# An order pinned, loads moved, a search moved and two priorities set in an attention-and-mixer kernel

## The chip, the cores and the metric

The kernel runs on one core of a Trainium2 chip. The metric is the device time of one execution in microseconds (us), as a median of several runs. Names in use below: PE is TensorE (matrix products), DVE is VectorE, ACT is ScalarE, POOL is GpSimd, and SP is SyncE, which issues most DMAs.

## The reference

For each of eight batches, an attention with two parts is computed from q, k and v (8 heads, 576 positions, width 64), and its result x goes through two pairs of products with a relu between, one along the positions and one along the channels:

```python
B, H, S, D = q.shape              # 8, 8, 576, 64
q_d = q.reshape(B, H, Sd, 4, D).mean(axis=3)      # likewise k_d, v_d; Sd = 144
out_d = sm_attn(q_d, k_d, v_d)                    # softmax attention, pooled
out_up = np.repeat(out_d, 4, axis=2)
mask = np.abs(pos[:, None] - pos[None, :]) < 4    # local attention
out_local = softmax(where(mask, scale * q @ k.T, -1e9)) @ v
x = (out_up + out_local), as (B, S, 512)

h = np.maximum(x.T @ w_tok1, 0.0) @ w_tok2        # (512,576)(576,256), (256,576)
u = x + h.T
h2 = np.maximum(u @ w_ch1, 0.0) @ w_ch2           # (576,512)(512,1536), (1536,512)
return u + h2
```

## The kernel before

The products run in 16-bit pairs: a float32 operand is split into a high and a low half after scaling by the largest value found, and three matmuls take the place of one. Each batch passes through these steps: loads of q, k (tiles `qk`), v (tiles `vr`, eight pieces of 72 x 512) and the windows of v (`vw`); pooling of q and k on POOL (lines 513 to 521); for each piece of v a square on ACT whose accumulated sum goes into `vm` (line 484) and two additions on POOL into `vd` (lines 487, 488); `value_scale`, which searches the largest of `vm` (DVE, a transposition and a broadcast on PE, DVE again: lines 649 to 658, 307 to 317); the pooled attention (sd, pd, td, ad, od) and the local attention (sc, P, pT, av); the position products (t1, hid, t2), which leave u; then the channel products. u is scaled and split into `uh` (lines 755, 757), the first channel product makes h, the second makes c2, and line 1025 adds it into u, which goes out.

Batches 0 and 1 take the first channel product directly (`c1_...`, 12 chunks for each of two column ranges, ranges 0 and 1). From batch 2 on, `product7` makes it with seven block products instead of eight, for six pairs of chunks: products P, Q and R with operands named a11, s1, s2, a12, s4, s3 and a22 go into three PSUM banks (m0, m1, m2). ACT copies three of them out (x1, m5, u2: line 903, in `plain`), DVE adds later ones onto those (lines 945, 949, 954), and ACT's relu and DVE's rest put the results into h (lines 910, 916, in `leave` and `rests`). The seven products need sums and differences of the channel weights, which `weight_sums` (lines 973 to 1002) makes once while batch 1 runs: for each of six pairs four additions (line 984) and four subtractions (line 991) on DVE, four casts and four subtractions on POOL (lines 993, 994), and two stores to DRAM (`sums0` to `sums5`), which batch 2 begins to read.

What sets the order: the preparation of the weights, batch 0, and part of batch 1 and of the loading of batches 1 and 2 is laid out by `drive`, which weighs planned durations, inside a stretch where the framework keeps the written order. All that follows is written by the loop at lines 1119 to 1163: each product step of PE with some work for the next batch beside it. The framework's scheduler then puts each engine's instructions into an order of its own, by dependences and priority; an instruction is free to move ahead unless `tc.keep_in_program_order` holds it. Every engine, and SP's queue, then works through its list in that order.

Tiles come from pools with a number of slots each. A tag "w" has four slots, one tile each, which `slot` picks in turn outside of `drive`; inside `drive` it returns the slot in use last. Pieces of v of batches 2 and later, and the tiles pd and ptd of the pooled attention, are in these slots. The loading of v stands thus:

```python
early = {0: 8, 1: 5}.get(st.b, 0)
for i in range(8):
    if i >= early:
        fetch(i)
    t = ts.pop(i)
    nc.scalar.activation(dump, t..., AF.Square, ..., accum_out=st.vm[:, i:i + 1])   # line 484
    nc.gpsimd.tensor_add(...); nc.gpsimd.tensor_add(st.vd..., ...)                  # lines 487, 488
```

Of the kernel before, what the change touches and what calls it, by code (L numbers as in the profile page):

```python
# [13 lines left out]
AF = mybir.ActivationFunctionType  # L14
# [14 lines left out]
LIVE = 3  # L29
# [14 lines left out]
def tile_ups_attention_mixer(ctx, tc, qk, vw, vr, w1, w2, c1, c2, out):  # L44
# [410 lines left out]
    def load_v(st):  # L455
# [17 lines left out]

        early = {0: 8, 1: 5}.get(st.b, 0)
        for i in range(early):
            yield step("S", ISSUE, *([("mixed", 0)] if st.b and i == 0 else []))
            fetch(i)
        for i in range(8):
            pr, g = divmod(i, 2)
            if i >= early:  # L480
                fetch(i)
            t = ts.pop(i)
            e = yield step("A", 0.7, at=arrives[i])
            nc.scalar.activation(dump, t.rearrange("p r c -> p (r c)"), AF.Square, scale=2.0 ** -20, accum_out=st.vm[:, i:i + 1])  # L484
            make(("vm", st.b, i), e)
            e = yield step("G", 1.25)
            nc.gpsimd.tensor_add(t[:, 0:2], t[:, 0:2], t[:, 2:4])  # L487
            nc.gpsimd.tensor_add(st.vd[:, g, 2 * pr:2 * pr + 2, :D], t[:, 0].rearrange("p (h d) -> p h d", d=D),
                                 t[:, 1].rearrange("p (h d) -> p h d", d=D))
            make(("v", st.b, i), e)  # L490
# [328 lines left out]
    def attention(st):  # L819
        todo = [pooled(st, pr) for pr in range(4)] + [local(st, t) for t in range(len(TILES))]  # L820
        yield from together(todo, LIVE)

# [4 lines left out]
    def ahead(b):  # L827
# [6 lines left out]
        yield from load_v(st)  # L834
        yield from value_scale(st)
        if b == 1:
# [44 lines left out]
    def product7(st, steps):  # L881
# [19 lines left out]
        def plain(src, name, engine):  # L901
            t = T([128, HS], F32, "tm", f"{name}{b}_{p}")
            nc.scalar.copy(t, src[:, :HS])
            return t
# [3 lines left out]
        def leave(src, r, i, h):  # L908
            o = h[:, i, :, HS * r:HS * r + HS]
            nc.scalar.activation(o[:, 0], src, AF.Relu)  # L910
            later.append((src, o))

        def rests():
            while later:
                src, o = later.pop(0)
                nc.vector.scalar_tensor_tensor(o[:, 1], src, 0.0, o[:, 0], ALU.max, ALU.subtract)

# [4 lines left out]
        for p in range(NP):  # L922
# [21 lines left out]
            product(Q, "a12", weights(fa, 1), True, True)  # L944
            nc.vector.tensor_tensor(x1, x1, Q[:, :HS], ALU.add)
            leave(x1, 0, 0, h)
            yield step("P", us, ("uh", b, "s4"))
            product(R, "s4", weights(fb, 1), False, True)
            nc.vector.tensor_tensor(u2, u2, R[:, :HS], ALU.add)  # L949
            rests()  # L950
            leave(u2, 0, 1, h)
            yield step("P", us, ("uh", b, "s3"))
            product(P, "s3", weights(0, 0, t123, 2), False, False)
            nc.vector.tensor_tensor(m5, m5, P[:, :HS], ALU.add)
            rests()
# [17 lines left out]
    def weight_sums():  # L973
# [4 lines left out]
        for p in range(NF // 2):  # L978
            fa, fb = C1.fin[2 * p], C1.fin[2 * p + 1]
            y = {}  # L980
            for n, f, o in (("a1", fa, 0), ("b1", fb, 0), ("b2", fb, 256), ("a2", fa, 256)):
                yield step("V", 0.42, gates[p])
                y[n] = T([128, 256], F32, "tm", f"{n}_{p}")
                nc.vector.tensor_tensor(y[n], f[:, 0, o:o + 256], f[:, 1, o:o + 256], ALU.add)
            if p == 0:
                ts12 = T([128, 2, 2, 256], F16, "uh", "ts12")
                ts3 = T([128, 2, 256], F16, "uh", "ts3")
            for x, z, o in (("b1", "a1", ts12[:, 0]), ("b2", "b1", ts3), ("b2", "a1", ts12[:, 1]), ("a2", "b2", fb[:, :, 0:256])):
                yield step("V", 0.42)
                to = {("b1", "a1"): "a1", ("b2", "b1"): "b1", ("b2", "a1"): "b2", ("a2", "b2"): "a2"}[x, z]  # L990
                nc.vector.tensor_tensor(y[to], y[x], y[z], ALU.subtract)
                yield step("G", 1.5)
                nc.gpsimd.tensor_copy(o[:, 0], y[to])
                nc.gpsimd.tensor_sub(o[:, 1], y[to], o[:, 0])
                if o is ts3:
# [216 lines left out]
```

## Time and profile before

| | us |
|---|---|
| median of three runs | 961.62 (960.66 to 961.94) |
| the profiled execution | 963.37 |
| its span in the trace | 961.6 |
| PE busy | 892.8 (93%) |
| DVE, ACT, POOL busy | 538.3, 424.7, 300.2 |

The page lists for each engine how long it was busy, and for groups of instructions how long the engine had been idle before them and whose work ended that. Where PE is busy nearly always, the table by stage is the first to be read: the length of a stage less PE's busy time is what PE waited, and the column PEclk is the mean clock granted to it, 1.00 being the full 2.4 GHz and 0.50 the lower level of 1.2 GHz. The stages are: to 145 us weights and batch 0; to about 215 batch 0's second channel product; 215 to 287 batch 1's first channel product (column range 0, then 1); 287 to 332 its second; then for each batch from 2 on some 50 to 57 us of block products and some 52 us of the second product, with the next batch's attention and position products beside them; batch 2 starts at 347, batch 7 at 890.

### The profile page before, as it was taken

The page shows a single profiled execution, that of the slowest core. Times are in us where ns is not written, and L with a number is a line of the kernel's source. Part 1 is how long each engine was busy: PE and PEld are TensorE (multiplying, and loading weights), DVE is VectorE, ACT ScalarE, POOL GpSimd, SP SyncE. Part 2 cuts the span into 40 slices and gives each one's busy share as a digit, 9 for nine tenths or more (in the row PEclk, how much of TensorE's full clock was granted, in tenths as well). Part 3 has the DMA queues.
Part 4 walks back from the last instruction along what each step waited for, and adds up shares of the span by engine and source line. Part 5 has one row for each costly group of instructions (what it writes and reads, how often), then busy time and mean ns, then how long its engine had stood idle before and what let it go on. Part 6 is the DMA issues. An engine that isn't in the chain of part 4 may idle for free.

```text
span 961.6 us, 26341 instructions
## 1 busy us (share of the span) xinstructions
PE 892.8 (93%) x11218; PEld 660.7 (69%) x11218; DVE 538.3 (56%) x1287; ACT 424.7 (44%) x1004; POOL 300.2 (31%) x457
## 2 busy tenths in 40 slices
PE   7877899997889989999999999899999999999998
PEld 3544678676667757767777768667777768767786
DVE  7789886436772266623765266633755266624631
ACT  4755673434351156622664156522655155423520
POOL 5898940415674021342024121241015120002000
PEclk9768999998999979999999999999999999999999
DMA  9584331511225112250135102260135211100200
GB/s 269 171 276 143 120 80 44 170 45 39 71 80 168 42 41 75 84 173 19 41 108 168 53 29 79 75 180 18 41 107 157 57 36 52 53 20 19 65 27 32
DMA packets 35143, 84.87 MB, mean 88 GB/s; under 512 B 4273, under 2 KB 15537, under 8 KB 33777
## 3 DMA queue, kind: packets, MB, share of 16 engines
q1 hardware_dynamic: 32464, 80.82, 28.1%
q10 hardware_dynamic: 2560, 2.36, 0.9%
q8 instruction: 88, 1.44, 0.6%
q14 instruction: 31, 0.25, 0.1%
HBM read 69.01 MB, written 11.80 MB: 84 GB/s over the span
## 4 chain that ended last, share of the span: by engine, by line
PE 73%; DVE 16%; ACT 5%; issue 3%; DMA 1%; POOL 1%; ACTq 0%; POOLq 0%; DVEq 0%; SPq 0%
PE c L124 32%; PE t L124 10%; PE P L124 9%; PE R L124 4%; PE av L636 3%; PE ad L567 3%; PE sc L600 2%; PE t L702 2%; PE Q L124 2%; PE busy L168 2%; PE pT L623 2%; PE td L558 2%; PE sd L539 1%; DVE CX L239 1%; DVE uh L757 1%
## 5 line engine op out<-in xcount | busy, mean ns | idle before, releaser
L124 PE MATMUL c<-h,CX 128*128 128x320 f16 (+1 forms) x2304 | 310.0, 286 | 3.0 <-DVE u L949 2.0
L124 PEld LDWEIGHTS <-CX 128*128 128x128 f16 x2304 | 221.1, 98 | 66.9 <-issue 6.1
L124 PEld LDWEIGHTS <-CW 128*128 128x128 f16 x1440 | 137.9, 99 | 55.2 <-issue 17.7
L487 POOL TENSOR_TENSOR vr<-vr 72x256 f32<-72x256 f32 x64 | 52.6, 821 | 196.2 <-ACT dump L484 189.5
L1025 DVE SCALAR_TENSOR_TENSOR u<-c,io,u 128x256 f32<-128x256 f32 (+1 forms) x64 | 32.8, 513 | 95.9 <-PE c L124 95.7
L124 PE MATMUL c<-uh,CW 128*128 128x256 f16 (+1 forms) x576 | 82.3, 295 | 1.7 <-DVE h L878 1.7
L729 ACT ACTIVATE u<-t,down 128x256 f32<-128x256 f32 (+1 forms) x64 | 29.9, 498 | 121.1 <-PE t L124 121.1
L771 POOL TENSOR_TENSOR s<-u,u 128x288 f32<-128x288 f32 x12 | 9.3, 796 | 234.4 <-ACT u L729 234.4
L124 PEld LDWEIGHTS <-t 128*128 128x128 f16 x648 | 62.4, 99 | 23.6 <-issue 7.9
L731 DVE TENSOR_REDUCE umx<-u 128x1 f32<-128x256 f32 (+1 forms) x64 | 27.8, 451 | 89.0 <-ACT u L729 89.0
L513 POOL TENSOR_TENSOR qs<-qk 128x288 f32<-128x288 f32 x56 | 39.3, 701 | 94.5 <-DMA qk<-in_qk_dram 90.9
L680 DVE SCALAR_TENSOR_TENSOR xh<-x,back,xh 128x512 f16<-128x512 f32 (+1 forms) x40 | 33.0, 825 | 57.3 <-ACT xh L678 56.2
L124 PE MATMUL t<-xh,W 128*128 128x512 f16 (+1 forms) x240 | 60.1, 386 | 2.0 <-DVE xh L680 2.0
L124 PE MATMUL t<-W,hid 128*128 128x256 f16 (+1 forms) x384 | 60.2, 289 | 0.4
L641 ACT ACTIVATE x<-av,up 128x512 f32<-128x512 f32 (+1 forms) x40 | 27.3, 683 | 41.8 <-PE av L636 35.2
L484 ACT ACTIVATE dump<-vr 72x512 uint8<-72x512 f32 x64 | 40.0, 624 | 12.5 <-DMA vr<-in_vr_dram 11.8
L567 PE MATMUL ad<-vd,ptd 72*72 72x65 f32 x512 | 41.0, 235 | 4.5 <-issue 2.4
L567 PEld LDWEIGHTS ad<-vd,ptd 72*72 72x72 f32 x512 | 38.7, 150 | 8.3 <-issue 2.7
L551 ACT ACTIVATE pd<-sd,nmd 72x144 f32<-72x144 f32 x128 | 38.7, 377 | 12.6 <-DVE nmd L546 10.6
L124 PEld LDWEIGHTS <-hid 128*128 128x128 f16 x384 | 34.9, 99 | 11.1 <-ACT hid L716 1.8
L678 ACT ACTIVATE xh<-x,back 128x512 f16<-128x512 f32 (+1 forms) x40 | 28.8, 721 | 29.6 <-PE t L124 27.4
L636 PE MATMUL av<-vw,pt 47*32 47x64 f32 x2304 | 36.5, 234 | 5.4 <-DMA vw<-od 3.4
(182 smaller groups left out, 1595.6 us busy)
## 6 DMA issues: line engine op xcount, KB each, us to landing
qk<-in_qk_dram SPq DMA_DIRECT2D x32, 579.0 KB
t<-sums SPq DMA_DIRECT2D x36, 384.0 KB
vw<-in_vw_dram SPq DMA_DIRECT2D x32, 351.0 KB
vr<-in_vr_dram SPq DMA_DIRECT2D x64, 144.0 KB
C_raw<-in_c_dram SPq DMA_DIRECT2D x16, 512.0 KB
out_dram<-u SPq DMA_DIRECT2D x32, 160.0 KB
C_raws<-in_c_dram SPq DMA_DIRECT2D x8, 512.0 KB
out_dram<-u SPq DMA_DIRECT2D x32, 128.0 KB
```

What stands on the lines that cost most here:

```text
L124: nc.tensor.matmul(ps, lhs(a), rhs(c), start=first and i == 0, stop=last and i == 2, **kw)
L484: nc.scalar.activation(dump, t.rearrange("p r c -> p (r c)"), AF.Square, scale=2.0 ** -20, accum_out=st.vm[:, i:i + 1])
L487: nc.gpsimd.tensor_add(t[:, 0:2], t[:, 0:2], t[:, 2:4])
L513: nc.gpsimd.tensor_add(two, x[:, :, 0:2], x[:, :, 2:4])
L551: nc.scalar.activation(pd[:, par, g], s[:, par, g], AF.Exp, bias=nm[:, par, g:g + 1], scale=0.125 / 16)
L567: nc.tensor.matmul(ps[:, g, par], pt[:, par, kg, G * g:G * g + G], st.vd[:, kg, 2 * pr + par], start=kg == 0, stop=kg == 1)
L636: nc.tensor.matmul(ps[QB * j:QB * j + QB, par, D * hp:D * hp + D], pt[p, hp, QB * j:QB * j + QB], st.vw[h][p, g, D * hp:D * hp + D], start ...
L678: nc.scalar.activation(st.xh[t][:, 0], xf(t), AF.Copy, scale=back[:n])
L680: nc.vector.scalar_tensor_tensor(st.xh[t][:, 1], xf(t), back[:n], st.xh[t][:, 0], ALU.mult, ALU.subtract)
L729: nc.scalar.activation(st.u[c][:, s0:s0 + N], banks[ch, c // 2][:, c % 2, :N], AF.Copy, scale=st.down)
L731: nc.vector.tensor_reduce(st.umx[:, ch, c:c + 1], st.u[c][:, s0:s0 + N], axis=AX.X, op=ALU.max, apply_absolute_value=True)
L1025: nc.vector.scalar_tensor_tensor(u, banks[c, ch], io[:, ch:ch + 1], u, ALU.mult, ALU.add)
```

## The change

It has four parts. (1) The 96 instructions of the weight sums are held in the order in which they are written. (2) From batch 2 on, v is loaded two pieces ahead, and the squares are held in written order outside of `drive`. (3) From batch 2 on, `value_scale` leaves `ahead` and stands first among the generators of `attention`, where one more may be live. (4) The copies of `plain` and the three additions get priority 400, the relus and rests 300.

```diff
-        early = {0: 8, 1: 5}.get(st.b, 0)
+        early = {0: 8, 1: 5}.get(st.b, 2)
         for i in range(early):
-            yield step("S", ISSUE, *([("mixed", 0)] if st.b and i == 0 else []))
+            yield step("S", ISSUE, *([("mixed", 0)] if st.b == 1 and i == 0 else []))
             fetch(i)
         for i in range(8):
             pr, g = divmod(i, 2)
-            if i >= early:
+            if st.b < 2 and i >= early:
                 fetch(i)
+            if st.b > 1 and i + 2 < 8:
+                fetch(i + 2)
             t = ts.pop(i)
             e = yield step("A", 0.7, at=arrives[i])
-            nc.scalar.activation(dump, t.rearrange("p r c -> p (r c)"), AF.Square, scale=2.0 ** -20, accum_out=st.vm[:, i:i + 1])
+            square = nc.scalar.activation(dump, t.rearrange("p r c -> p (r c)"), AF.Square, scale=2.0 ** -20,
+                                          accum_out=st.vm[:, i:i + 1])
+            if st.b > 1 and not driven[0]:
+                tc.keep_in_program_order(square)
...
     def attention(st):
-        yield from together(todo, LIVE)
+        yield from together([value_scale(st)] + todo, LIVE + 1)
...
         yield from load_v(st)
-        yield from value_scale(st)
+        if b == 1:
+            yield from value_scale(st)
...
         def plain(src, name, engine):
-            nc.scalar.copy(t, src[:, :HS])
+            with tc.high_priority(400):
+                nc.scalar.copy(t, src[:, :HS])
...
         def leave(src, r, i, h):
-            nc.scalar.activation(o[:, 0], src, AF.Relu)
+            with tc.high_priority(300):
+                nc.scalar.activation(o[:, 0], src, AF.Relu)
...
-                nc.vector.scalar_tensor_tensor(o[:, 1], src, 0.0, o[:, 0], ALU.max, ALU.subtract)
+                with tc.high_priority(300):
+                    nc.vector.scalar_tensor_tensor(o[:, 1], src, 0.0, o[:, 0], ALU.max, ALU.subtract)
...
-            nc.vector.tensor_tensor(x1, x1, Q[:, :HS], ALU.add)
+            with tc.high_priority(400):
+                nc.vector.tensor_tensor(x1, x1, Q[:, :HS], ALU.add)
...
-                nc.vector.tensor_tensor(y[to], y[x], y[z], ALU.subtract)
+                tc.keep_in_program_order(nc.vector.tensor_tensor(y[to], y[x], y[z], ALU.subtract))
                 yield step("G", 1.5)
-                nc.gpsimd.tensor_copy(o[:, 0], y[to])
-                nc.gpsimd.tensor_sub(o[:, 1], y[to], o[:, 0])
+                tc.keep_in_program_order(nc.gpsimd.tensor_copy(o[:, 0], y[to]))
+                tc.keep_in_program_order(nc.gpsimd.tensor_sub(o[:, 1], y[to], o[:, 0]))
```

The additions onto u2 and m5 and the four additions of the sums are changed in the same way. In the changed file the lines stand 2 to 13 further down: the square is line 486, the copy 910, the relu 918, the rest 925, the additions 955, 960 and 966, the sums 997 and 1004.

The order of DVE's list, some 69 us into the program, where the channel weights (CW) are scaled and split and xh0 of batch 0 is made. Before the change:

```order
L363 SCALAR_TENSOR_TENSOR CW0_145<-CW1_146,C1_s0_135,CW0_145 128x512
L239 SCALAR_TENSOR_TENSOR CW8_153<-C17_raw_796 128x512
L984 TENSOR_TENSOR a1_0_3610<-CW0_145 128x256
L680 SCALAR_TENSOR_TENSOR xh0_2_1068<-x0_2_1050,back_129,xh0_2_1068 128x512
L363 SCALAR_TENSOR_TENSOR CW1_146<-CW2_147,C1_s0_135,CW1_146 128x512
L239 SCALAR_TENSOR_TENSOR CW10_155<-C19_raw_838 128x512
L984 TENSOR_TENSOR b1_0_3615<-CW1_146 128x256
L680 SCALAR_TENSOR_TENSOR xh0_2_1068<-x0_3_1063,back_129,xh0_2_1068 128x512
```

The same place of DVE's list after the change:

```order
L363 SCALAR_TENSOR_TENSOR CW0_145<-CW1_146,C1_s0_135,CW0_145 128x512
L239 SCALAR_TENSOR_TENSOR CW8_153<-C17_raw_796 128x512
L685 SCALAR_TENSOR_TENSOR xh0_2_1068<-x0_2_1050,back_129,xh0_2_1068 128x512
L363 SCALAR_TENSOR_TENSOR CW1_146<-CW2_147,C1_s0_135,CW1_146 128x512
L239 SCALAR_TENSOR_TENSOR CW10_155<-C19_raw_838 128x512
L685 SCALAR_TENSOR_TENSOR xh0_2_1068<-x0_3_1063,back_129,xh0_2_1068 128x512
```

The two sums a1_0 and b1_0 (line 984) are gone from here; nine more of lines 984 and 991 are gone from the list's next 25 places, and the sums now begin behind chunk 4 of batch 1's column range 1.

The order of ACT's list, where batch 1's position product leaves u1_0 to u1_3, which are scaled into uh1_0_0 and uh1_0_2 for its first channel product, and the pieces vr2_0 to vr2_7 of batch 2's v are squared. Before the change:

```order
L484 ACTIVATE dump_128,vm2_2939<-vr2_0_2941 72x512
L729 ACTIVATE u1_0_2874<-t2_1_1_0_2970,down1_2143 128x320
L729 ACTIVATE u1_1_2907<-t2_1_1_0_2970,down1_2143 128x320
L484 ACTIVATE dump_128,vm2_2939<-vr2_1_2986 72x512
L755 ACTIVATE uh1_0_0_3036<-u1_0_2874,us1_0_3006 128x256
L729 ACTIVATE u1_2_2943<-t2_1_1_2_3007,down1_2143 128x320
L755 ACTIVATE uh1_0_0_3036<-u1_1_2907,us1_0_3006 128x256
L729 ACTIVATE u1_3_2966<-t2_1_1_2_3007,down1_2143 128x320
L755 ACTIVATE uh1_0_2_3069<-u1_2_2943,us1_0_3006 128x256
L484 ACTIVATE dump_128,vm2_2939<-vr2_2_3040 72x512
L755 ACTIVATE uh1_0_2_3069<-u1_3_2966,us1_0_3006 128x256
```

The same place of ACT's list after the change:

```order
L734 ACTIVATE u1_0_2874<-t2_1_1_0_2969,down1_2143 128x320
L486 ACTIVATE dump_128,vm2_2939<-vr2_0_2967 72x512
L734 ACTIVATE u1_1_2907<-t2_1_1_0_2969,down1_2143 128x320
L486 ACTIVATE dump_128,vm2_2939<-vr2_1_2983 72x512
L760 ACTIVATE uh1_0_0_3040<-u1_0_2874,us1_0_3006 128x256
L734 ACTIVATE u1_2_2941<-t2_1_1_2_3007,down1_2143 128x320
L556 ACTIVATE pd2_0_3228<-sd2_0_3175,nmd2_0_3181 72x144 x4
L486 ACTIVATE dump_128,vm2_2939<-vr2_2_2985 72x512
L760 ACTIVATE uh1_0_0_3040<-u1_1_2907,us1_0_3006 128x256
L486 ACTIVATE dump_128,vm2_2939<-vr2_3_3023 72x512
L734 ACTIVATE u1_3_2964<-t2_1_1_2_3007,down1_2143 128x320
L760 ACTIVATE uh1_0_2_3083<-u1_2_2941,us1_0_3006 128x256
```

The square of vr2_0 stands one place further down, behind u1_0; those of vr2_2 and vr2_3 now stand ahead of u1_3; the last part of uh1_0_2 (from u1_3) has moved down to behind the square of vr2_5.

The order of DVE's list at the end of batch 4's block products, where the additions onto x1, u2 and m5 (named x14, u24, m54) and the rests into h4_5 stand beside batch 5's local attention (P, r5, mx5, xh5). Before the change:

```order
L945 TENSOR_TENSOR x14_4_8506<-x14_4_8506,Q_4_5_8615 128x288
L619 TENSOR_TENSOR P2_112<-P2_112,r5_1_8642 128x8x38
L612 TENSOR_TENSOR P0_110<-P0_110,mx5_2_8647 128x8x38
L680 SCALAR_TENSOR_TENSOR xh5_0_8978<-x5_0_8579,back_129,xh5_0_8978 128x512
L949 TENSOR_TENSOR u24_5_8573<-u24_5_8573,R_4_5_8557 128x288
L916 SCALAR_TENSOR_TENSOR h4_5_8556<-x14_4_8506,h4_5_8556 128x288
L954 TENSOR_TENSOR m54_5_8564<-m54_5_8564,P_4_4_8499 128x288
```

The same place of DVE's list after the change:

```order
L955 TENSOR_TENSOR x14_4_8502<-x14_4_8502,Q_4_5_8546 128x288
L960 TENSOR_TENSOR u24_5_8538<-u24_5_8538,R_4_5_8522 128x288
L966 TENSOR_TENSOR m54_5_8529<-m54_5_8529,P_4_4_8495 128x288
L925 SCALAR_TENSOR_TENSOR h4_5_8515<-x14_4_8502,h4_5_8515 128x288
L925 SCALAR_TENSOR_TENSOR h4_5_8515<-u24_5_8538,h4_5_8515 128x288
L925 SCALAR_TENSOR_TENSOR h4_5_8515<-m54_5_8529,h4_5_8515 128x288
L925 SCALAR_TENSOR_TENSOR h4_5_8515<-P_4_4_8495,h4_5_8515 128x288
```

The three additions now follow each other, with the four rests behind them, and the steps of batch 5's attention have left this place.

## Rows read from the trace of the kernel before

**Rows 1.** The page, busy time and share of the span of each engine.

```profile
PE 892.8 (93%) x11218; PEld 660.7 (69%) x11218; DVE 538.3 (56%) x1287; ACT 424.7 (44%) x1004; POOL 300.2 (31%) x457
```

**Rows 2.** Table by stage: stretch, length, busy us (and count) of each engine, clock, DMA.

```profile
core 0: us, PE busy (x) PEld busy (x) DVE busy (x) ACT busy (x) POOL busy (x), PEclk, DMA share, GB/s
0.00:145.00 145.00, 118.64 (x1423) 78.81 (x1423) 121.72 (x267) 89.74 (x197) 108.87 (x139) 0.87 0.58 176
215.00:247.00 32.00, 27.16 (x307) 22.29 (x306) 20.61 (x55) 15.01 (x44) 13.12 (x22) 0.89 0.10 32
247.00:287.00 40.00, 32.91 (x585) 23.97 (x583) 31.69 (x73) 17.55 (x43) 31.75 (x53) 0.91 0.27 85
287.00:332.00 45.00, 45.00 (x458) 33.21 (x457) 11.14 (x22) 7.97 (x14) 10.09 (x21) 1.00 0.38 115
...
347.00:890.00 543.00, 521.26 (x6816) 389.94 (x6816) 287.05 (x709) 245.35 (x597) 117.82 (x190) 0.99 0.26 74
```

**Rows 3.** The same for DVE's line 984 alone, 69 to 89.5 us.

```profile
69.00:89.50 20.50, 3.28 (x6) 0.82 0.43 142
```

**Rows 4.** The same for DVE's line 991 alone, 69 to 89.5 us.

```profile
69.00:89.50 20.50, 3.32 (x5) 0.82 0.43 142
```

**Rows 5.** PE's waits by releaser, 69 to 100 us: us in total, times, longest.

```profile
PE C_sum L393 <- DVE CX L239: 3.1, 3, 1.8
PE t L124 <- DVE xh L680: 2.0, 2, 1.1
```

**Rows 6.** Chain of waits in 60 to 145 us, shares by line.

```profile
by line: PE c L124 28.2%; DVE CX L239 9.9%; DVE CW L363 8.7%; issue 7.4%; DVE uh L757 4.8%; DVE CW L239 4.2%; PE t L124 3.7%; DVE xh L680 2.9%; DVE a L991 2.6%; PE ad L567 2.4%; DVE umx L731 1.9%; ACT u L729 1.8%; DVE b L984 1.8%; PE C_sum 
```

**Rows 7.** PE's waits, 215 to 287 us.

```profile
PE vm_t L652 <- DVE vm_m L649: 4.8, 1, 4.8
PE pT L623 <- DVE od L575: 3.9, 1, 3.9
```

**Rows 8.** Timeline of DVE, two sums of line 991.

```profile
229.90 0.60 DVE L991 TENSOR_TENSOR a<-a,b 128x256 f32<-128x256 f32 x1
...
231.80 0.42 DVE L991 TENSOR_TENSOR a<-b,a 128x256 f32<-128x256 f32 x1
```

**Rows 9.** Timeline of POOL, a subtraction and a cast, idle time between in brackets.

```profile
229.55 0.67 POOL L994 TENSOR_TENSOR ts<-b,ts 128x256 f16<-128x256 f32 x1
232.42 0.40 POOL L993 CAST ts<-a 128x256 f16<-128x256 f32 x1 [2.20 <-DMA sums<-ts]
```

**Rows 10.** Timeline of SyncE's loads of v: start, length, line, instruction, count.

```profile
205.40 9.80 SPq L471 DMA_DIRECT2D vr<-in_vr_dram  x3
...
219.53 0.30 SPq L471 DMA_DIRECT2D vr<-in_vr_dram  x1
```

**Rows 11.** Timeline of ACT there, idle time before and its end in brackets.

```profile
207.11 0.95 ACT L729 ACTIVATE u<-t,down 128x320 f32<-128x320 f32 x2 [3.34 <-PE t L124]
...
217.35 0.63 ACT L484 ACTIVATE dump<-vr 72x512 uint8<-72x512 f32 x1 [3.53 <-DMA vr<-in_vr_dram]
```

**Rows 12.** Timeline of PE, start of batch 1's product.

```profile
214.95 1.47 PE L124 MATMUL c<-uh,CW 128*128 128x256 f16 x12
```

**Rows 13.** PE's waits, 332 to 347.5 us.

```profile
PE um_b L658 <- DVE um_m L655: 1.9, 1, 1.9
```

**Rows 14.** PE's waits, 347 to 890 us.

```profile
PE P L124 <- DVE m L954: 5.0, 5, 1.7
PE Q L124 <- DVE h L916: 3.8, 5, 0.8
...
PE P L124 <- ACT x L903: 2.1, 4, 0.8
PE c L124 <- DVE u L949: 2.0, 2, 1.0
```

**Rows 15.** Timeline of DVE, end of batch 4's block products.

```profile
612.59 0.61 DVE L916 SCALAR_TENSOR_TENSOR h<-x,h 128x288 f16<-128x288 f32 x1
613.12 0.44 DVE L954 TENSOR_TENSOR m<-m,P 128x288 f32<-128x288 f32 x1
```

More of the change, by code (lines that the diff above doesn't have):

```diff
@@ L948, in product7 @@
             product(R, "s4", weights(fb, 1), False, True)
-            nc.vector.tensor_tensor(u2, u2, R[:, :HS], ALU.add)
+            with tc.high_priority(400):
+                nc.vector.tensor_tensor(u2, u2, R[:, :HS], ALU.add)
             rests()
@@ L953, in product7 @@
             product(P, "s3", weights(0, 0, t123, 2), False, False)
-            nc.vector.tensor_tensor(m5, m5, P[:, :HS], ALU.add)
+            with tc.high_priority(400):
+                nc.vector.tensor_tensor(m5, m5, P[:, :HS], ALU.add)
             rests()
@@ L983, in weight_sums @@
                 y[n] = T([128, 256], F32, "tm", f"{n}_{p}")
-                nc.vector.tensor_tensor(y[n], f[:, 0, o:o + 256], f[:, 1, o:o + 256], ALU.add)
+                tc.keep_in_program_order(
+                    nc.vector.tensor_tensor(y[n], f[:, 0, o:o + 256], f[:, 1, o:o + 256], ALU.add))
             if p == 0:
```

## The prediction

> **What bounds the kernel now.** I read first the page's busy shares, then the table by stage, then what TensorE (PE) waited for in each stage, and last the timelines around the longest waits. PE is busy 93% of the span [rows 1], so a change can give back only PE's idle time and time at the lower clock. The table by stage [rows 2] shows where that lies. The first 145 us have 145.0 - 118.6 = 26.4 us of PE idle. From 215 to 287 us (batch 1's first product) there are 4.8 + 7.1 us at a mean granted clock of 0.89 and 0.91; of two levels, 0.5 and 1.0, that makes 0.22 x 32 = 7.0 us and 0.18 x 40 = 7.2 us at 1.2 instead of 2.4 GHz, each costing half, 3.5 us. Batch 1's second product (287 to 332) has none. From 347 to 890, the periods of batches 2 to 6, 543.0 - 521.3 = 21.7 us are idle, at full clock but for one stretch. The change touches all of these.
>
> **Part 1, the weight sums pinned.** The first order fence shows something that the diff does not say: sums stand among VectorE's (DVE's) weight preparation, long before their emitted place. Between 69.0 and 89.5 us there are six of line 984 and five of line 991, 3.28 + 3.32 = 6.6 us [rows 3, 4]. PE waits for DVE there: 3.1 us for CX, 2.0 us for xh [rows 5]. The chain of waits of 60 to 145 us charges 2.6% and 1.8% to lines 991 and 984, 4.4% of 85 us = 3.7 us [rows 6]. In the changed order all eleven are gone and the rest of DVE's list there is the same. They can give 0 (if GpSimd, POOL, or a load is late next) to 6.6 us; I take two thirds of the chain's 3.7, since other engines stand close behind. **Term A: -2.5 us, from -6.6 to 0.**
>
> The rest of the sums stood in batch 1's first product. There PE waits 3.9 us for od of DVE (transposes pT) [rows 7]; the idle of 247 to 287 is 7.1 us in all and its clock costs 3.5 us [rows 2]. In the changed order the sums begin behind the fifth of that product's second dozen of chunks and go on into the second product. **Term C: -7 us of these 10.6, from -10.6 to -3**, because eight sums and some waits of the attention still stand there.
>
> The second product of batch 1 then carries them. DVE is busy 11.1 of its 45 us [rows 2]; 48 sums at 0.42 to 0.60 us [rows 8] add 20 to 29 us, so it still has room. POOL has 10.1 of 45 and gets 24 casts of 0.40 us and 24 subtractions of 0.67 us [rows 9], 25.7 us. POOL does the pooling of batch 3's q and k, its 10.1 us, between them in list order. By a walk of the changed order the sums of four of six blocks, 16 x 1.07 = 17 us, the pooling, and some 14 us until its loads are in, make 41 us until DVE comes to the next evacuation that PE needs; PE is there some 45 us after the sums begin. **Term D: 0, from 0 to +6.**
>
> On those rows a rule can be weighed: a sum took 0.60 us at 229.90 while POOL was at work, and 0.42 us at 231.80 [rows 8] while POOL was idle [rows 9]. The Trainium skill, "SBUF — State Buffer", section "Who interferes with whom", says that VectorE and GpSimd share a port pair and that a VectorE operation with two SBUF inputs and a GpSimd operation that reads SBUF exclude each other, the second one waiting for the whole of the first. The trace agrees in direction, with 0.2 us rather than a whole operation. If it held in full, the moved sums would get in each other's way; that is the third rival below.
>
> **Part 2, squares of v pinned, loads two ahead.** Batch 2's eight pieces of v all use one slot of the pool w, so that "two ahead" cannot be: in the changed program each load waits for the additions of the piece before. The profile shows the price of a link: three issues in 9.80 us of which the last takes about 0.3 us, so (9.80 - 0.3) / 2 = 4.75 us each, and the next one at 219.53 [rows 10]. Before, four pieces went one after another at this pace in this stretch. Now all eight do, and the second order fence shows whose way they are in on ScalarE (ACT): the square of piece 0 stands behind u1_0 (207.11 + 0.48 = 207.6 us [rows 11]), the squares of pieces 2 and 3 ahead of u1_3, and piece 5's ahead of the last part of uh1_0_2, which PE needs for the first chunks of batch 1's product. Piece 5 comes at 207.6 + 5 x 4.75 = 231.4; with its 0.63 us [rows 11], 0.5 us for uh and the same on DVE, PE goes on at 233. It began these chunks at 214.95 [rows 12] and has some 4 us of other work ordered ahead of that point: about 13 us of idle. Against that the 4.8 us for the largest v [rows 7] and the 3.5 us of clock of 215 to 247 fall away, while the long idle brings lower clock of its own, some 2.5 us. **Term B: 13 - 8.3 + 2.5 = +7 us, from 0 (if the loads land sooner when nothing else is on the queue) to +13.**
>
> From batch 3 on four slots serve, pieces 0 to 3 are loaded well ahead, and the squares stand in the second product, where ACT is little used. I cost them at 0; the cover is that stage's idle ACT (8.0 of 45 us [rows 2]). If it fails, a link of 4.75 us per batch is the price.
>
> **Part 3, the largest v later.** At 347 the head of batch 2's product waits 1.9 us for a search of a maximum [rows 13]; the later value scale takes another search out of DVE's list there. **Term E: -1.5 us, from -3 to +1.** In later batches the scale's two small PE steps stand in the product's first blocks behind three evacuations of DVE: 0 to 0.8 us per batch, inside the next term's range.
>
> **Part 4, priority for emptying block products.** In 347 to 890 PE waits for exactly the instructions that are raised: 5.0 us for m of line 954, 3.8 us for h of 916, 2.1 us for x of 903, 2.0 us for u of 949 [rows 14], 12.9 of the 21.7 us. The third order fence and [rows 15] show one: the a22 product waits up to 1.7 us for that m, in batch 4 for the addition at 613.12, which stood behind a relu rest (0.61 us) and, ahead of that, xh and attention work. Now the three additions stand in a row, nothing of the attention among them, and the next product's first chunk is ahead of a22 on PE. The squares (0.63 us each [rows 11]) have left ACT's list there too. I take three quarters of 12.9. **Term F: -10 us, from -12.9 to -4.** What is late next is td on ACT's exponentials, which no part touches.
>
> **The sum.** -2.5 + 7 - 7 + 0 - 1.5 - 10 = -14 us. The profiled execution took 963.37 us for a span of 961.6, 1.75 us above the median of the runs, 961.62. So 949.4 us in such an execution, and 947.6, say 948 us, as a median.
>
> **The rivals.**
> 1. *The pinned squares hold ACT in every batch.* For it: the ACT list keeps them in place whatever arrives, batch 2's chain does just that, and pieces 4 to 7 still need slots that the pooled attention uses. Against: four slots and a long second product. One link of 4.75 us in each of batches 3 to 7 is 23.8 us, which gives 948 + 24 = 972 us. It decides the sign from 14 / 5 = 2.8 us per batch on. Chance 0.12.
> 2. *The priorities only move waits.* PE's product blocks depend on each other through three PSUM banks; an addition that comes sooner makes a relu later, which Q of the next block waits for. Then F is near -2: 956 us. For it: [rows 14] has 3.8 us on just that relu. Chance 0.2.
> 3. *The sums crowd batch 1's second product.* With 0.2 us more for each of POOL's 48, POOL ends 10 us later, the squares of batch 3 that wait behind its last loads hold ACT's evacuations, and PE loses up to that: 958 us. The port rule of the Trainium skill, cited above, would work in this way. Chance 0.12.
> 4. *Gains only where the sums left, B at its upper end.* -2.5 + 13 - 4 - 0 - 5 = +1.5: 963 us, no measurable change. Chance 0.06.
>
> **How the numbers follow.** My forecast has 0.5. About 0.2% is what a measurement here can tell from no change, 1.9 us, so faster means under 959.7. Forecast, rival 2 and nearly all of rival 3 make 0.80; rival 4 and what is left of 3 make 0.07; rival 1, and B with F both at their bad ends, 0.13. For the range I leave rival 1 and half of rival 4 out above: 961 us. Below, A, C and F at their better ends together give -4.1 - 3.6 - 2.9 = 10.6 us more: 937 us.
>
> **What would show it.** In the profile after: no line of the sums before some 245 us, and the 69 to 100 us waits for CX and xh shorter (A); an ACT wait for loads of v at 212 to 232 and PE idle of over 8 us there (B); no wait of 3 us for od near 257 (C); no PE idle in batch 1's second product (D); waits for lines 954, 903 and 949 (now at other numbers) under 3 us in all after 347 (F). I am wrong if squares of v end ACT's idle time for over 3 us in later batches, if PE waits at 287 to 347, or if the waits for the relu rests grow by what the additions give.

## The result, and the profile after

Over fifteen runs of each kernel the median went from 962.5 us (959.9 to 966.3) to 953.97 us (948.2 to 960.9), a ratio of 0.9911 with a 95% interval of 0.9886 to 0.9936. 948 us was forecast, with 937 to 961 as its range: faster, as forecast, with 8.5 us gained where 13.6 (961.62 to 948) were expected.

The profiled execution took 949.53 us, at the fast end of those runs. Its page, to be set beside [rows 1]:

```profile
span 947.8 us, 26409 instructions
...
PE 887.2 (94%) x11218; PEld 659.0 (70%) x11218; DVE 529.5 (56%) x1287; ACT 423.6 (45%) x1004; POOL 297.2 (31%) x457
```

The table by stage, with the same columns as [rows 2], is cut where the same PE work begins: batch 1's first channel product from its range 0 (with what PE does while that waits) and range 1, its second product with the attention behind it, the last steps ahead of batch 2's first block product, and batches 2 to 6.

```profile
205.10:251.40 46.30, 36.48 (x406) 27.04 (x404) 19.27 (x55) 19.50 (x55) 9.44 (x16) 0.85 0.09 27
251.40:279.50 28.10, 27.68 (x490) 20.93 (x489) 16.99 (x45) 10.56 (x22) 4.59 (x9) 1.00 0.24 75
279.50:328.60 49.10, 46.94 (x499) 34.49 (x497) 34.70 (x68) 14.35 (x32) 41.68 (x70) 1.00 0.43 129
328.60:342.10 13.50, 11.20 (x86) 7.83 (x84) 5.31 (x19) 3.48 (x10) 8.35 (x13) 1.00 0.31 97
342.10:875.90 533.80, 518.22 (x6822) 391.28 (x6822) 277.46 (x713) 243.53 (x597) 114.64 (x190) 0.99 0.25 75
```

The first row is the one to look at: 46.3 us with only 36.5 us of PE busy, and a granted clock of 0.85. The last row, 533.8 us for the five periods, answers to 542.7 us (347.0 to 889.7) before. The rows of the kernel before that answer to the first, the second and the last:

```profile
208.70:246.50 37.80, 32.96 (x350) 26.42 (x348) 23.45 (x62) 18.15 (x52) 15.41 (x26) 0.91 0.10 31
246.50:286.70 40.20, 33.11 (x588) 24.07 (x585) 32.19 (x73) 17.44 (x43) 31.70 (x53) 0.92 0.27 85
347.00:889.70 542.70, 520.96 (x6814) 389.69 (x6814) 286.75 (x709) 245.05 (x596) 117.52 (x190) 0.99 0.26 74
```

Stage by stage, each from the first instruction of one mark to that of the next, in the two profiled executions:

| from, to | before | after | difference | forecast |
|---|---|---|---|---|
| start, last tile of batch 0's second product | 208.7 | 205.1 | -3.6 | A -2.5 |
| that, range 1 of batch 1's first product | 37.8 | 46.3 | +8.5 | B +7 |
| that, batch 1's second product | 40.2 | 28.2 | -12.1 | C -7 |
| that, batch 2's first block product | 60.3 | 62.6 | +2.3 | D 0, E -1.5 |
| batches 2 to 6 | 542.7 | 533.8 | -8.9 | F -10 |
| batch 7 | 71.9 | 71.9 | 0 | |

The sum is -13.8 us and was forecast as -14. That the fifteen runs gave less is not visible in this one trace.

Term A's mechanism can be read from the sums' first and last start, by line and form (duration minimum, median, maximum in ns, then first and last start in us); before, line 984 began at 69.1:

```profile
L997 DVE TENSOR_TENSOR a<-CW x12: 406/598/892, 263.7 to 317.6; 128x256 f32<-128x256 f16 x12
L997 DVE TENSOR_TENSOR b<-CW x12: 407/504/945, 265.7 to 316.7; 128x256 f32<-128x256 f16 x12
```

The waits for DVE in 69 to 100 us, which were to become shorter, did so for CX and not for xh (columns as in [rows 5]):

```profile
PE t L124 <- DVE xh L685: 3.2, 2, 1.9
PE C_sum L393 <- DVE CX L239: 2.2, 3, 1.4
```

Term B's is read on three engines. SyncE's loads of batch 2's v (columns as in [rows 10]), where three issues took 9.80 us before:

```profile
205.98 27.84 SPq L471 DMA_DIRECT2D vr<-in_vr_dram  x7
```

ACT's squares and the instructions behind them, with the idle time ahead and what ended it:

```profile
217.55 0.63 ACT L486 ACTIVATE dump<-vr 72x512 uint8<-72x512 f32 x1 [3.47 <-DMA vr<-in_vr_dram]
...
218.17 0.51 ACT L734 ACTIVATE u<-t,down 128x320 f32<-128x320 f32 x1
...
226.83 0.63 ACT L486 ACTIVATE dump<-vr 72x512 uint8<-72x512 f32 x1 [1.29 <-DMA vr<-in_vr_dram]
...
227.46 0.49 ACT L760 ACTIVATE uh<-u,us 128x256 f16<-128x256 f32 x1
```

and PE at the same time:

```profile
209.62 0.38 PE L124 MATMUL c<-uh,CW 128*128 128x256 f16 x2 [2.09 <-ACT uh L760]
...
218.82 0.47 PE L544 MATMUL sd<-qd 64*72 64x144 f32 x4 [2.38 <-ACT u L734]
...
228.01 0.59 PE L124 MATMUL c<-uh,CW 128*128 128x256 f16 x2 [3.98 <-ACT uh L760]
```

Seven issues in 27.84 us are (27.84 - 0.3) / 6 = 4.6 us a link, where the forecast had 4.75. ACT sits in front of the square at 217.55 for 3.5 us; u1_3 (line 734) follows it at 218.17, and PE, which had waited 2.4 us for that u, goes on at 218.82. The square at 226.83 is piece 5; uh1_0_2 follows at 227.46, and PE starts at 228.01 after 4.0 us. In all ACT waits for loads of v (waits of ACT, 205 to 240 us: total, times, longest):

```profile
ACT dump L486 <- DMA vr<-in_vr_dram: 15.5, 7, 3.5
```

### The profile page after: what moved, and what is told of

The parts are those of the page before. It is cut to its first block, busy times and chain, and to the rows that moved or that the text cites. A ratio compares the mean times of both kernels' runs of the same rounds, so it can differ in the third digit from the quotient of the medians.

```text
span 947.8 us, 26409 instructions
## 1 busy us (share of the span) xinstructions
PE 887.2 (94%) x11218; PEld 659.0 (70%) x11218; DVE 529.5 (56%) x1287; ACT 423.6 (45%) x1004; POOL 297.2 (31%) x457
## 4 chain that ended last, share of the span: by engine, by line
PE 75%; DVE 14%; DMA 4%; ACT 3%; issue 3%; POOL 1%; ACTq 0%; POOLq 0%; DVEq 0%
PE c L124 31%; PE t L124 10%; PE P L124 9%; PE R L124 5%; PE ad L572 3%; PE av L641 3%; PE Q L124 2%; DMA vr<-in_vr_dram 2%; PE t L707 2%; PE sc L605 2%; PE pT L628 2%; PE td L563 2%; DMA vw<-od 1%; PE busy L168 1%; PE sd L544 1%
## 5 line engine op out<-in xcount | busy, mean ns | idle before, releaser
L1038 DVE SCALAR_TENSOR_TENSOR u<-c,io,u 128x256 f32<-128x256 f32 (+1 forms) x64 | 32.8, 513 | 103.8 <-PE c L124 103.6
L518 POOL TENSOR_TENSOR qs<-qk 128x288 f32<-128x288 f32 x56 | 43.9, 784 | 137.8 <-DMA qk<-in_qk_dram 134.2
L492 POOL TENSOR_TENSOR vr<-vr 72x256 f32<-72x256 f32 x64 | 47.7, 745 | 113.2 <-ACT dump L486 112.5
L124 PEld LDWEIGHTS <-W 128*128 128x128 f16 (+1 forms) x240 | 22.6, 99 | 29.4 <-issue 9.8
```

The lines of the kernel that those rows point to most:

```text
L124: nc.tensor.matmul(ps, lhs(a), rhs(c), start=first and i == 0, stop=last and i == 2, **kw)
L518: nc.gpsimd.tensor_add(two, x[:, :, 0:2], x[:, :, 2:4])
L1038: nc.vector.scalar_tensor_tensor(u, banks[c, ch], io[:, ch:ch + 1], u, ALU.mult, ALU.add)
```

## The experiments

Rival theories stood against each other for each large term. For the start of batch 1's product: the chain of loads through one slot costs the time, or the place of the squares in ACT's list does, or the time is only moved. For batches 2 to 6: the priorities shorten them, as forecast, or what leaves ACT and DVE there does.

**Each part alone** (e1 to e4). The kernel before with one part of the change. First the pinned sums:

```diff
-                nc.vector.tensor_tensor(y[n], f[:, 0, o:o + 256], f[:, 1, o:o + 256], ALU.add)
+                tc.keep_in_program_order(
+                    nc.vector.tensor_tensor(y[n], f[:, 0, o:o + 256], f[:, 1, o:o + 256], ALU.add))
... (likewise line 991, and POOL's cast and subtraction)
```

> The kernel before with the weight sums pinned and nothing else. Terms A, C and D of the prediction: the preparation ends 2.5 to 4 us sooner, batch 1's first product loses 7 us or more of idle and lower clock, its second product gains 0 to 3 us. Theory: 949 to 954 us. If the sums only carry their cost into the second product (third rival): 958 us or more.

Measured: 953.71 us, ratio 0.989 (0.9856 to 0.9924). The single largest part, then. Its last tile of batch 0's second product began at 206.2 us (208.7 before), and batch 2's first block product at 336.6 instead of 347.0. A wait for DVE's attention work remains in batch 1's first product, larger than the 3.9 us of [rows 7]:

```profile
PE pT L623 <- DVE P L619: 5.0, 3, 2.5
PE vm_t L652 <- DVE vm_m L649: 2.4, 1, 2.4
```

so in this kernel term C did not work as told, by a wait that vanishes: pT still waits. From the first instruction of range 1 to the second product the idle time went from 7.1 to 5.6 us and the length from 40.2 to 35.8: more of the gain is PE's busy time, 30.3 us for as many matmuls as took 33.1 before, at a clock of 1.00 instead of 0.92. The row of that stage:

```profile
240.40:276.30 35.90, 30.25 (x589) 22.08 (x587) 25.47 (x60) 17.94 (x43) 19.04 (x30) 1.00 0.21 54
```

The second product of batch 1 stayed at 45.0 us with no PE idle; the third rival has nothing for it here.

The priorities alone:

```diff
-            nc.scalar.copy(t, src[:, :HS])
+            with tc.high_priority(400):
+                nc.scalar.copy(t, src[:, :HS])
... (likewise the additions at 400, relus and rests at 300)
```

> The kernel before with the two priorities and nothing else. If term F is theirs: waits for lines 954, 903 and 949 under 3 us in batches 2 to 6, and 952 to 955 us. If the priorities only move waits (second rival): 959 to 962 us, with the waits for relu rests grown. If F needs the squares out of the way too: 955 to 959 us.

Measured: 963.32 us, ratio 1.0019 (0.9996 to 1.0043). No gain. Yet PE's waits in batches 2 to 6 look as term F wanted them. The list no longer holds m of line 954 or h of 916; new are the transposes pT, which wait for DVE's softmax P:

```profile
PE pT L623 <- DVE P L619: 3.4, 8, 0.6
PE av L636 <- issue: 3.1, 2, 2.4
PE td L558 <- ACT pd L551: 2.9, 4, 0.8
PE P L124 <- DVE x L949: 1.8, 3, 0.8
```

PE's idle time fell, and PE's busy time rose by nearly as much. The stage (347 to 886 us) of this kernel:

```profile
346.70:886.30 539.60, 523.37 (x6814) 389.37 (x6814) 285.41 (x709) 242.99 (x596) 120.58 (x190) 0.99 0.25 74
```

against the same stage of the kernel with only the sums pinned, where the order of these batches is that of before and the waits of [rows 14] stand at 4.9, 3.9, 2.2 and 2.1 us:

```profile
336.60:875.70 539.10, 518.46 (x6813) 388.91 (x6813) 285.89 (x709) 244.86 (x596) 117.36 (x190) 1.00 0.26 74
```

539.6 - 523.4 = 16.2 us idle against 539.1 - 518.5 = 20.6, for the same length and nearly the same number of matmuls. Idle time saved was not time saved here: PE's busy time rose by 4.9 us. The clock column differs too (0.99 against 1.00, at most 0.01 x 540 = 5 us of it); what else made PE busy for longer is not shown.

The loads two ahead and the squares pinned, alone:

```diff
-        early = {0: 8, 1: 5}.get(st.b, 0)
+        early = {0: 8, 1: 5}.get(st.b, 2)
...
+            if st.b > 1 and i + 2 < 8:
+                fetch(i + 2)
...
+            if st.b > 1 and not driven[0]:
+                tc.keep_in_program_order(square)
```

> The kernel before with the loads of v two pieces ahead and the squares pinned, nothing else. Theory (term B): batch 1's product starts 7 to 13 us late behind batch 2's chain of loads, and the later batches gain 0 to 4 us: 964 to 972 us. If the squares hold ACT in every batch (first rival): over 980 us. If the chain costs PE nothing net: 957 to 962 us.

Measured: 966.79 us, ratio 1.0034 (1.0018 to 1.005). Slower, inside the theory's figures. Its batch 2 begins at 359.2 us, 12 us late, and its batches 2 to 6 take 535.2 us, 7.5 us less than before. The first rival (over 980 us) is out: after 250 us ACT has no wait for a load of v, neither in this trace nor in that of the changed kernel. The kernel before has eight there, 7.6 us in all.

The search of the largest v later, alone:

```diff
-        yield from together(todo, LIVE)
+        yield from together([value_scale(st)] + todo, LIVE + 1)
...
-        yield from value_scale(st)
+        if b == 1:
+            yield from value_scale(st)
```

> The kernel before with the search of the largest v later and nothing else. Term E: 959 to 962 us, no measurable change. If the search in the block products costs PE 0.8 us a batch: 965 us.

Measured: 965.65 us, ratio 1.0037 (1.0013 to 1.006). A small loss, near the rival's 965. Its profiled execution (960.1 us of span, some 4 us under its median) shows no step at which it could be read; batches 2 to 6 were 538.8 us in it. Where the loss lies stays open.

**The load chain taken away** (e5, e9). Twice, in two ways. First the changed kernel with batch 2's loads in the order of before:

```diff
-        early = {0: 8, 1: 5}.get(st.b, 2)
+        early = {0: 8, 1: 5, 2: 0}.get(st.b, 2)
...
-            if st.b < 2 and i >= early:
+            if st.b < 3 and i >= early:
                 fetch(i)
-            if st.b > 1 and i + 2 < 8:
+            if st.b > 2 and i + 2 < 8:
                 fetch(i + 2)
```

> The changed kernel with batch 2's pieces of v loaded and squared in the order of the kernel before; the later batches as changed. It takes away the chain of eight loads ahead of u1_3. If that chain is what costs the changed kernel about 11 us at the start of batch 1's product (term B): PE idle of at most 5 us in that product, and 940 to 947 us. If the time was only moved (the head of batch 2's product or the sums' stage is late instead): 950 to 955 us.

Measured: 938.32 us, ratio 0.975 (0.9722 to 0.9778), below both expected ranges. The start of batch 1's product and batches 2 to 6:

```profile
206.10:238.90 32.80, 30.58 (x406) 24.96 (x404) 19.17 (x54) 18.30 (x53) 8.38 (x14) 1.00 0.07 20
...
330.50:862.50 532.00, 518.04 (x6822) 391.89 (x6822) 278.00 (x713) 243.91 (x597) 114.55 (x190) 0.99 0.25 75
```

The first row has as many matmuls, 406, as the 46.3 us of the changed kernel, in 32.8 us: 2.2 us idle instead of 9.8, and PE busy 30.6 us instead of 36.5, at a clock of 1.00 instead of 0.85. The chain cost 13.5 us in that execution, 7.6 of idle and 5.9 of clock; in medians 953.97 - 938.32 = 15.7 us. Nothing was given back later on balance: range 1 took 31.1 us instead of 28.2, but the two stages behind it 60.5 and 532.0 instead of 62.6 and 533.8.

Then the changed kernel with four slots for those loads, the squares left where the change puts them:

```diff
+            elif tag == "w" and driven[0]:
+                ts[i] = sb.tile([G, 4, 128], F32, tag=f"w{i % 4}", name=f"vr{st.b}_{i}", bufs=1)
             else:
                 ts[i] = T([G, 4, 128], F32, tag, f"vr{st.b}_{i}")
```

> The changed kernel with one line more: batch 2's pieces of v take the four slots of w in turn. The squares of pieces 2 and 3 still stand ahead of u1_3, so the order stays about as changed, but a load waits for the piece four before it. If the single slot makes the cost of term B: PE idle at the start of batch 1's product under 3 us at full clock, and 934 to 942 us, as with the loads as before. If the place of the squares alone costs: 948 us or more.

Measured: 937.58 us, ratio 0.9737 (0.9701 to 0.9773). The squares of pieces 2 and 3 still stand ahead of u1_3 in its ACT list. SyncE's seven issues now take 8.4 us:

```profile
202.10 8.36 SPq L473 DMA_DIRECT2D vr<-in_vr_dram  x7
```

and the stage, up to the first instruction of range 1, has 0.5 us of PE idle at full clock:

```profile
205.50:236.90 31.40, 30.95 (x406) 24.76 (x404) 18.86 (x55) 18.59 (x54) 9.18 (x16) 1.00 0.09 25
```

That is 31.4 us for the 406 matmuls that took the changed kernel 46.3. So it was the slot and not the place: a square whose data is there costs its 0.63 us, one whose data is 4.6 us away costs the engine that waits behind it.

**The changed kernel less one part** (e6 to e8). Without the pinned sums:

```diff
-                tc.keep_in_program_order(nc.vector.tensor_tensor(y[to], y[x], y[z], ALU.subtract))
+                nc.vector.tensor_tensor(y[to], y[x], y[z], ALU.subtract)
... (all four forms)
```

> The changed kernel with the weight sums left to the scheduler. Pinning alone gave 0.989. If it is worth the same within the changed kernel: 963 to 967 us, with sums back among the weight preparation and the wait for od near 257 us. If the other parts had given it anyway: under 957 us.

Measured: 968.17 us, ratio 1.0051 (1.0025 to 1.0076), just above the first range: 14 us lost, where the pinned sums alone (e1) were worth 9. Sums stand among the weights again, and PE waits in the second half of batch 1's first product (255 to 301 us):

```profile
PE c L124 <- DVE h L884: 4.0, 1, 4.0
PE ad L572 <- DVE od L580: 2.5, 1, 2.5
```

Without the priorities (`with tc.high_priority(...)` taken out at all six places):

> The changed kernel without the two priorities. Alone they gave nothing (1.002). If they are worth something once the squares are out of ScalarE's way: 957 to 960 us. If the squares' and the search's new place are what shortens batches 2 to 6: 952 to 956 us, the same as the changed kernel.

Measured: 951.8 us, ratio 0.9888 (0.9846 to 0.993), the same as the changed kernel's 0.9911. Its five periods took 530.7 us. The row for its start of batch 1's product shows that the chain is not worth the same in each execution:

```profile
209.80:258.90 49.10, 38.27 (x405) 28.63 (x402) 19.25 (x55) 19.23 (x55) 9.59 (x16) 0.83 0.09 25
```

49.1 us for 405 matmuls where the changed kernel's trace had 46.3 for 406: 10.8 us idle instead of 9.8, clock 0.83 instead of 0.85.

Without the later search (`value_scale` back in `ahead`, `together(todo, LIVE)` in `attention`):

> The changed kernel with the search of the largest v back at the end of the loading of each batch. Alone its move gave 1.004. If it costs within the changed kernel too: 949 to 952 us. If the block products need it out of the way: 956 to 960 us.

Measured: 958.23 us, ratio 0.9953 (0.9921 to 0.9986). By the medians the later search is worth some 4 us here, though alone it lost 3; the intervals of e8 and of the changed kernel overlap (0.9921 to 0.9936), so the 4 us are not certain.

The parts do not add up. Alone they made -8.7 (e1), +0.9 (e2), +4.4 (e3) and +3.2 us (e4) in medians, together -0.2; the changed kernel, with all four, made -8.5.

**What shortens batches 2 to 6** (e10 to e12). Three more. The first is the kernel of the first chain experiment without the priorities:

```diff
-            with tc.high_priority(400):
-                nc.scalar.copy(t, src[:, :HS])
+            nc.scalar.copy(t, src[:, :HS])
... (and the five others)
```

> Batch 2's loads as before, sums pinned, squares of later batches pinned, search later, but without the two priorities. The changed kernel did not miss them (0.989 against 0.991). If that holds: 936 to 941 us. If they are worth something where nothing else is late: 943 us or more.

Measured: 937.98 us, ratio 0.9739 (0.9705 to 0.9773): the same with them or without.

The kernel before with the later batches' squares and loads as changed and the search later (its diff is that of e12 below and that of e4 above together):

> The kernel before with the later batches' squares and loads as changed and the search later, batch 2's loads as before, no pinned sums and no priorities. If these two together make what was forecast for the priorities (term F, batches 2 to 6 some 9 us shorter): 951 to 956 us. If they gain only with the priorities or the sums: 960 us or more.

Measured: 950.13 us, ratio 0.9885 (0.9831 to 0.9939), 1 us under the first range, which its interval reaches into.

And with those squares and loads alone:

```diff
-        early = {0: 8, 1: 5}.get(st.b, 0)
+        early = {0: 8, 1: 5, 2: 0}.get(st.b, 2)
...
-            if i >= early:
+            if st.b < 3 and i >= early:
                 fetch(i)
+            if st.b > 2 and i + 2 < 8:
+                fetch(i + 2)
...
+            if st.b > 1 and not driven[0]:
+                tc.keep_in_program_order(square)
```

> The kernel before with the later batches' squares and loads as changed and nothing else. By the stages of the earlier runs the squares alone shorten batches 2 to 6 by 2 to 5 us: 956 to 960 us. If they need the search out of the way: 961 to 964 us. If they carry the whole gain: 951 to 955 us.

Measured: 954.07 us, ratio 0.9913 (0.9887 to 0.9938), the case in which the squares carry the whole gain. Batches 2 to 6:

```profile
343.90:878.10 534.20, 519.86 (x6814) 388.45 (x6814) 280.35 (x709) 244.90 (x596) 110.48 (x190) 1.00 0.26 75
```

534.2 us, against 542.7 before. The waits that were to be the priorities' prey are nearly all still there, in total, times and longest:

```profile
PE Q L124 <- DVE h L921: 3.9, 5, 0.8
PE P L124 <- DVE m L959: 3.4, 5, 0.7
PE P L124 <- ACT x L908: 3.0, 5, 0.8
PE R L124 <- DVE u L954: 1.7, 4, 0.4
```

They are 12.0 us, where the four of [rows 14] are 12.9: nearly all of the gain came without them. In all PE's idle time fell from 21.7 to 14.3 us. Among what is gone is a wait of the kernel before for ACT's exponentials, which no part of the change raises (347 to 890 us):

```profile
PE td L558 <- ACT pd L551: 2.8, 4, 0.8
```

In the changed kernel, where the search is later too, that wait stands again at 2.8 us, so it is not the whole of the gain.

The squares themselves left the block products. In the kernel before, 25 of the 32 squares that stand in the periods of batches 2 to 5 ran between a batch's first block product and its second product, among the relus and copies; in this one none does. ACT's time for the squares in these four stretches, before (347.0 to 396.8, 455.9 to 503.5, 564.0 to 614.5 and 675.2 to 723.6 us) and in e12:

```profile
sum 196.30, ACT 17.40; mean ACT 4.35
...
sum 191.00, ACT 0.00; mean ACT 0.00
```

Whether the earlier loads or the held order moved them was not tested apart, and how the 17.4 us of ACT reach PE was not followed further.

Against the same part with batch 2's chain (e3, 966.79 us) e12 is 12.7 us less, the chain's price once more.

Put together, batches 2 to 6 took in the fourteen profiled executions:

| | us |
|---|---|
| neither squares nor search moved (before, e1, e2) | 542.7, 539.2, 539.6 |
| search only (e4) | 538.8 |
| squares only (e3, e12; with priorities e8) | 535.2, 534.2; 538.6 |
| both, without priorities (e7, e10, e11) | 530.7, 533.8, 534.2 |
| both, with priorities (after, e5, e6, e9) | 533.8, 532.0, 530.1, 534.9 |

The last two rows have means of 532.9 and 532.7 us. Single values differ by up to 4.8 us within a row, so a part's own 2 or 3 us cannot be read off one pair; the step from the first row (mean 540.5) to the last two can. In e8 the 538.6 us are long by PE's busy time (524.6 us, in e12 519.9) and not by its idle time, which is 14.0 us, close to e12's 14.3 and e3's 15.3.

## Why the prediction was right, and where it was wrong

**Sign and sum** were right, within the range; the profiled execution was forecast to 0.1 us (949.4, measured 949.53). Much of that is luck. The terms missed by -1.1 (A), +1.5 (B), -5.1 (C), +3.8 (D and E) and +1.1 us (F), and these cancel. And the median lies 4.4 us above that execution, while the profiled execution of the kernel before lies 0.9 us above its own median of 962.5. Its sister without the priorities (e7), with the same chain, spends 49.1 us in the stage where it spent 46.3, and began the last tile of batch 0's second product 4.7 us later (209.8 against 205.1). Whether the other fourteen runs lost their time at these two places is not shown: no second trace of the changed kernel itself was taken.

**Term A** (-2.5) was right in cause and a little small. The last tile of batch 0's second product began at 205.1 to 209.8 us in the seven profiles with pinned sums (mean 206.8) and at 208.7 to 212.9 in the seven without (mean 210.8): -4.0 us. The sign by which I wanted to see it, shorter waits for xh, failed for xh (3.2 us instead of 2.0), so that the two together stayed at 5.4 us after 5.1. The idle time ahead of batch 0's first channel product fell from 25.7 to 24.1 us and PE's clock differs too; through which of its waits the four us came is not shown.

**Term B** (+7) was right in mechanism: the chain, its price per link (4.75 told, 4.6 measured), the squares named and the instructions behind them. Its size was a composition of two errors that offset each other. I put PE's new idle time at 13 us (233 - 214.95 - 4 is rather 14), and it was 9.8 in all: piece 5 was squared at 226.83 instead of 231.4, and parts of c1 and sd stood in the holes (the rows at 209.62 and 218.82). And I put the lower clock of the stage at 2.5 us, where the comparison with e5 gives 5.9 (30.6 to 36.5 us busy for as many matmuls), and with e7's 38.3 us 7.7. The step that failed is the price of idle time at the clock. Net of work that moved, the chain took 13.5 us in the trace and 15.7 in medians.

**Term C** (-7, measured -12.1) was right in what it names: the idle time of range 1 fell from 7.1 to 0.4 us, and its clock rose from 0.92 to 1.00. It was mis-sized because a part of the work was misplaced: 56 matmuls more were done ahead of the cut than before (406 against 350), and 32 more behind range 1. The same 56 stand ahead of it in e4, where only the search is later, and none in e3, where only the loads and squares are changed: this is part 3's doing, which the prediction did not see. So B to E are better taken together: forecast -1.5, measured -1.3 in the trace, and +1.6 in e7.

**Terms D and E** (0 and -1.5, measured +2.3 together): PE does wait in batch 1's second product where it did not, for pT on the softmax in DVE's list (columns as in [rows 7]):

```profile
PE pT L628 <- DVE P L624: 2.1, 2, 1.2
```

The third rival is thus there in small, with 2.2 us of idle, one of the prediction's own signs of being wrong; the 32 matmuls that moved here are in the +2.3 too. Term E's gain is hardly there: PE's waits for searches at the head of batch 2's product were 2.5 us before (1.9 + 0.6) and are 1.8 now. POOL was busy 41.7 of 49.1 us, more than the 10.1 + 25.7 I had counted. What POOL costs a sum can be read from pairs like this one:

```profile
302.50 0.72 POOL L1007 TENSOR_TENSOR CW<-a,CW 128x256 f16<-128x256 f32 x1
302.62 0.89 DVE L1004 TENSOR_TENSOR b<-b,b 128x256 f32<-128x256 f32 x1
```

When the sum starts, POOL's subtraction has 302.50 + 0.72 - 302.62 = 0.60 us to go, and the sum takes 0.89 us, which is 0.29 more. Of the 48 sums of this trace 14 start with POOL idle and take 0.41 to 0.43 us. Of the other 34, 30 take what POOL's operation has left plus 0.28 us, within 0.03, or 0.41 us where that is less; the other four, beside the pooling of line 518, take 0.41 us. The sum of [rows 8] at 229.90 fits too: POOL had 229.55 + 0.67 - 229.90 = 0.32 us to go, and it took 0.60. The Trainium skill, "SBUF — State Buffer", section "Who interferes with whom", would have the second of two such operations wait for the whole of the first. The trace agrees for these 30 of 34. So the prediction read its rows wrongly when it found "0.2 us rather than a whole operation": little of POOL's operation was left. The rule held nearly in full, and yet PE lost only the 2.2 us above. The medians of the sums stayed where they were (0.60 and 0.50 us of line 997, before 0.59 and 0.66 of line 984), since sums met POOL before the change too.

**Term F** (-10, measured -8.9) had the right size for the wrong reason, and that is the main error. The step that failed was "in 347 to 890 PE waits for exactly the instructions that are raised", read as: raising them gives the time. e2, e7 and e10 say the priorities give nothing (1.0019 alone, 0.9888 without them against 0.9911 with, 0.9739 against 0.975). e12 says that the later batches' squares and loads give nearly all of it, -8.5 us in the trace and -9.1 in medians, with the waits still standing. I had costed these squares at 0 and named them only as helpers. Some of the -8.9 is spread between executions: e1, whose batches 2 to 6 stand in the order of the kernel before, took 539.2 us and not 542.7. Term F's own sign, waits for the raised lines of under 3 us, came true (1.7 us for the x addition, 0.5 for the x copy), and so does not tell what gave the time. PE's longest waits after:

```profile
PE av L641 <- issue: 3.4, 2, 3.1
PE td L563 <- ACT pd L556: 2.8, 4, 0.8
PE P L124 <- DVE x L955: 1.7, 3, 0.7
PE pT L628 <- ACT pt L632: 1.6, 5, 0.3
```

The second rival, that the priorities only move waits, was true of the priorities (chance given: 0.2), but its price was wrong, since the time came from part 2 at the same place.

**Rival 1** was wrong from batch 3 on, as said above (e3); in batch 2 it is term B.

Three versions are well ahead of both kernels: the changed one with batch 2's loads as before (0.975), that without priorities (0.9739), and the changed one with four slots (0.9737). Their intervals overlap; the third changes least.

## What to carry to other kernels

A wait names the instruction that came last, not what made it late: before a priority is set for the named one, try to take the unneeded work out of its engine's list. Where an in-order list has an instruction whose data comes through a chain of loads, count the slots first; "two ahead" with one slot puts every link in front of whatever stands behind it. And an order that a scheduler fills freely can put work of a later stage into an earlier stage that is short of that engine, so look for each moved line's first start, not only at the place where it was written.

## What was not expected of the hardware

In the changed kernel idle time in short pieces cost nearly as much again in clock. In its stage 205 to 251 us PE had holes of 2.1, 2.4 and 4.0 us, and the granted clock was 0.85 in the mean, that is the lower level of 1.2 GHz for 0.15 / 0.5 x 46.3 = 13.9 us; in e5 as many matmuls ran at 1.00, with 7.6 us less idle and 5.9 us less busy. That is no fixed price: range 1 of the kernel before had 7.1 us of idle at a clock of 0.92, which is 0.08 x 40.2 = 3.2 us lost.

The runs of the changed kernel spread from 948.2 to 960.9 us over fifteen, those of the version with four slots from 933.5 to 940.2 over four. The holes do not explain that: e3, with the same chain of loads, spread from 963.8 to 969.1 over ten, and e11, without it, from 947.6 to 959.6 over four.

A sum on DVE that started while POOL was at work took what POOL's operation had left plus 0.28 us, in 30 of 34 cases (terms D and E).
